# Softmax reciprocal on ScalarE, eight residuals by accumulating stores, and a third pairwise add of the logit products, in a fused attention-plus-GeGLU kernel

## Chip, cores and metric

The kernel runs on one core of one Trainium2 chip. The metric is the device time of one execution in microseconds, lower is better. Three runs of the kernel before gave 183.99, 184.02 and 184.84 us, the median is 184.02 us.

## What is computed

The input x has 2048 rows of 512 bfloat16 values. Its layer norm goes through two parallel branches, and both results are added to x:

```
xn = layernorm(x)
q, k, v = split(xn @ wqkv)                 # 32 heads of 16
logits[h, s, w] = q[h, s] . k[h, s - 2*w] / 4      # w = 0..7, masked where s - 2*w < 0
o[h, s] = sum over w of softmax_w(logits)[h, s, w] * v[h, s - 2*w]
A = o @ wo
B = (gelu(xn @ w_gate) * (xn @ w_up)) @ w_down      # inner width 1376
out = x + A + B
```

## The kernel before

**Tiling.** The 2048 rows are worked on in four blocks of 512 (b = 0 to 3), each of four tiles of 128 rows. Activations lie transposed (features on partitions, 512 rows along the free dimension), and matmuls are 128x128 by 128x512 in bfloat16 into one of eight PSUM banks.

**Names.** Every piece of work is a task with a name, a block number b and often a tile number. The tasks that matter here, with the engine that runs them:

- TensorE: `mm{b}_{0,1,2}_{g}` (line 1009) makes Q, K and V in four groups g; `fg{b}_{j}` and `fu{b}_{j}` (1217) make gate and up columns; `er{b}_3` (1085) sums the logit products over the partitions of a head by a matmul with a 0/1 matrix; `acc..{t}` (1302) makes the output tile t from both branches, in one bank. The parts `accw12` to `accw15` are the attention share of the last block and are kept for the end.
- ScalarE: `evq`, `evk`, `evv` (1020), `gelu` (1227), `uev` (1234) and `fe` (1335) empty PSUM banks; `exp{b}` (1131) is the exponential of the softmax; `bnst`, `bnag`, `sub`, `norm` and small ones are the layer norm of later blocks.
- VectorE: `pr{b}_{g}` (1040) multiplies Q by eight shifted copies of K (4096 elements per partition, float16); `pa{b}_0` and `pa{b}_1` (1053) add the four products in pairs; `d1`, `d2` (1117, 1122) subtract the maximum of the logits; `d4a`, `d4b`, `d4c` (1138) sum the eight exponentials; `d5` (1150) is the reciprocal of that sum; `d6` (1155) multiplies; `pv`, `pw`, `pz` (1184, 1193, 1199) weight V and sum into OT; `h` (1241) multiplies gelu by up; `fin` (1340, 1346) adds the residual x.
- SyncE issues all DMAs: loads, `ss`/`sl` (1164, 1176), which send the softmax weights to DRAM and bring them back spread over partitions, the transposing `trx` (882), the residual loads `ldxr` (1288) and the stores `sto` (1353).
- GpSimd makes constants at the start and a power per pair of tiles (`sq`, 832).

**What sets the order.** The order of the tasks on each engine is written out by hand in `ORDER` (line 404), one list for each engine, and each engine runs its list strictly in sequence. `Graph.schedule` (207) only gives out the buffer slots in that order, and `assign_sync` (317) puts semaphore waits where a task reads, overwrites or reuses what another engine made. So a task that waits holds back everything behind it on its engine. Buffers that tie the engines together are the eight PSUM banks (the two of the logits are held from `er` to `exp`), three slots each for gelu and up tiles (freed by `h`), and four output tiles OB (written by `fe`, freed when the store has landed).

**The softmax of one block** runs `er` on TensorE, `d1` and `d2` on VectorE, `exp` on ScalarE, `d4a`, `d4b`, `d4c`, `d5`, `d6` on VectorE, then `ss`, `sl`, `pv`, `pw`, `pz`. In the third and fourth block, as in the others, `er` takes two rounds of eight matmuls, one for each pair sum:

```
hhs = (0,) if b in PR_ADD3 else (0, 1)
```

with `PR_ADD3` empty. ScalarE works from tables of functions: gelu and exp lie in different ones, and a switch is an instruction of its own, which the build puts ahead of the first activation that needs it. The kernel before has ten such loads.

**Residuals.** For each of the 16 output tiles SyncE loads 128 rows of x (`ldxr`), `fe` copies the bank to OB (14 tiles), `fin` adds x on VectorE, and SyncE stores the tile (`sto`).

Of the kernel before, what the change touches and what calls it, by code (L numbers as in the profile page):

```python
# [12 lines left out]
    DMA_ISSUE=0.48,  # L13
    DMA_FIXED=2.0,
# [121 lines left out]
class Graph:  # L136
# [70 lines left out]
    def schedule(self, orders, params=None):  # L207
# [59 lines left out]
        for _ in range(len(self.tasks)):  # L267
# [23 lines left out]
            elif t.eng == "pe":  # L291
                sw = 0.0
                if t.mode is not None:
                    if pe_mode not in (None, t.mode):
                        sw = prm["PE_MODE_SWITCH"]
                    pe_mode = t.mode
                t.end = est + sw + pe_clock.run(est, t.dur, t.util)
                t.done = t.end + prm["PE_DRAIN"]
            else:
                t.end = est + t.dur  # L300
                t.done = t.end + prm["DRAIN"]
                if t.eng == "act" and t.table is not None:
                    act_table = t.table
# [13 lines left out]
    def assign_sync(self, cnt_sems, dma_sems):  # L317
        order = self.order
        for e in ("pe", "act", "dve", "pool"):
            for i, t in enumerate(order[e]):  # L320
                t.seq = i + 1
                t.sem = cnt_sems[e]
                t.val = i + 1
# [3 lines left out]
        for t in order["sp"]:  # L327
# [6 lines left out]
            dlast[si] = t  # L334
        self.dma_totals = [(dma_sems[i], dcount[i]) for i in range(len(dma_sems)) if dcount[i] > 0]
        know = {e: {} for e in ENGS}
        allt = sorted((t for t in self.tasks if not t.dropped), key=lambda t: (t.start, t.idx))
        for t in allt:
            K = know[t.eng]
            deps = list(t.deps)  # L340
            if t.eng == "sp" and t.prev_on_sem is not None:
                deps.append(t.prev_on_sem)
# [21 lines left out]
    def emit_engine(self, eng_name, e):  # L364
# [7 lines left out]
        for t in self.order[eng_name]:  # L372
# [4 lines left out]
            if eng_name == "sp" and t is self.order["sp"][-4]:  # L377
                late = self.order["sp"][-7:]
                for (s, tot) in self.dma_totals:
# [3 lines left out]
            ins.then_inc(t.sem, 16 if eng_name == "sp" else 1)  # L383
# [5 lines left out]
    def report(self):  # L389
# [18 lines left out]
        "mm0_2_0_0 mm0_2_3_0 mm0_2_2_0 mm0_2_1_0 fg0_0 fg0_1 fg0_2 fu0_0 fg0_3 fu0_1 fu0_2 fg0_4 fu0_3 fg0_5 "  # L408
        "fu0_4 fu0_5 fg0_6 fg0_7 er0_3 mm1_0_0_0 mm1_1_0_0 mm1_0_1_0 mm1_1_1_0 fg1_0 fu0_6 mm1_0_3_0 "
        "mm1_0_2_0 mm1_1_3_0 fu0_7 fu1_0 fg1_1 fg0_8 fu1_1 mm1_1_2_0 fu0_8 mm1_2_0_0 fg1_2 fg0_9 fu1_2 "  # L410
        "mm1_2_2_0 fg1_3 fu1_3 fu0_9 fg0_10 fg1_4 fu1_4 mm1_2_3_0 fg1_5 mm1_2_1_0 fg1_6 fu1_5 fu1_6 fg1_7 "
        "mm2_0_0_0 mm2_1_1_0 mm2_1_0_0 mm2_0_3_0 er1_3 mm2_0_1_0 fg1_10 mm2_1_2_0 mm2_2_1_0 mm2_0_2_0 fu1_7 "
        "fg2_0 accd1 mm2_1_3_0 accd2 fg2_1 mm2_2_3_0 mm2_2_2_0 fg1_8 fg2_2 acca0 fu2_0 accb0 fg1_9 mm2_2_0_0 "
        "accd3 er2_3 fu2_1 fu1_8 fu1_9 fu2_2 fg2_3 fu2_3 mm3_1_2_0 mm3_1_1_0 mm3_1_3_0 mm3_0_1_0 mm3_0_0_0 "
        "fg2_4 mm3_1_0_0 fu2_4 mm3_0_2_0 fg3_0 mm3_0_3_0 fu3_0 fg3_1 fg2_10 fg3_2 accd7 accd5 mm3_2_0_0 "
        "fg2_5 fu3_1 fg3_3 mm3_2_3_0 mm3_2_1_0 fu2_5 fu3_2 acca4 er3_3 accb4 fg3_4 accd6 fu3_3 fu3_4 fg2_6 "
        "fg3_5 fu2_6 fg2_7 fg3_6 fu2_7 fg2_8 fu2_8 fu3_5 fg3_7 fu3_6 mm3_2_2_0 fg2_9 fu3_7 fu2_9 fg3_8 fu3_8 "
        "fg3_9 fg3_10 acca8 accd10 accd9 fu3_9 accb8 accd11 acca12 accd13 accd14_0 accd14_1 accw14_0 "
        "accw14_1 accw13 accb12 accd15_0 accw12 accw15_0 accd15_1 accw15_1 accd15_2 accw15_2",
    "act":  # L420
        "c_tbl sx1 sq0 negm1 sxx1 sq1 evx0_0 evx0_1 evq0_0 sq2 evq0_1 evk0_0 evx1_0 sq3 evk0_1 bnst8 evx1_1 "
        "bnst9 evq0_2 sq6 evk0_2 evq0_3 evk0_3 ve8 evv0_0_0 sq4 vp8 bnag8 bnag9 va8 gelu0_0 evv0_2_0 "
        "evv0_3_0 bnst10 gelu0_1 bnst11 uev0_2 gelu0_3 vb8 gelu0_4 uev0_1 uev0_3 ve10 gelu0_5 uev0_4 uev0_0 "
        "uev0_5 gelu0_2 halo1 vp10 gelu0_7 bnag10 bnag11 evq1_0_0 evk1_0_0 evv0_1_0 evq1_1_0 evk1_1_0 "
        "gelu0_6 exp0 sub11 evq1_3_0 evk1_3_0 evq1_2_0 va10 uev0_7 uev1_0 uev0_10c uev0_6 sub9 vb10 sub8 "
        "uev1_1 evk1_2_0 norm9 uev0_10b gelu1_1 gelu1_0 norm8 gelu0_8 evv1_0_0 gelu1_2 sub10 uev0_8 bnst12 "
        "gelu0_9 norm11 uev1_2 uev0_9 norm10 evv1_2_0 gelu1_4 gelu1_3 uev1_3 evv1_1_0 uev1_4 uev1_5 uev0_10a "
        "bnst13 gelu1_5 gelu0_10 uev1_6 evk2_1_0 evv1_3_0 evk2_0_0 ve12 vp12 gelu1_7 bnag12 evq2_0_0 gelu1_6 "
        "evq2_1_0 uev1_10b bnag13 uev1_10c halv1 evk2_2_0 evq2_2_0 halo2 exp1 bnst14 sub12 bnst15 uev1_7 "
        "va12 ve14 vb12 uev1_10a vp14 bnag14 evk2_3_0 bnag15 evq2_3_0 evv2_1_0 va14 vb14 fe1 fe2 sub14 "  # L430
        "gelu2_0 evv2_2_0 halo3 gelu1_10 sub15 uev2_0 norm12 sub13 evv2_0_0 evv2_3_0 norm13 fe0 norm15 fe3 "
        "norm14 gelu1_8 gelu2_1 gelu1_9 uev2_1 uev1_8 uev2_2 uev1_9 uev2_3 gelu2_2 evk3_2_0 evk3_1_0 "
        "uev2_10b gelu2_3 exp2 evq3_1_0 evk3_3_0 evq3_2_0 evq3_0_0 halv2 evk3_0_0 uev2_10c evq3_3_0 uev2_4 "
        "uev2_10a gelu2_10 gelu3_1 uev3_0 gelu3_0 fe7 evv3_0_0 gelu2_5 gelu3_3 evv3_1_0 uev2_5 uev3_1 fe5 "
        "gelu2_4 gelu3_2 uev3_10c halv3 evv3_3_0 uev3_2 fe4 fe6 uev3_3 uev3_10b exp3 gelu3_5 uev2_6 gelu3_4 "
        "gelu2_7 uev2_7 uev2_8 gelu3_6 gelu2_6 evv3_2_0 gelu3_7 uev3_4 gelu2_8 gelu2_9 uev2_9 uev3_10a "
        "uev3_7 uev3_5 uev3_6 gelu3_10 fe10 gelu3_8 gelu3_9 uev3_9 fe9 uev3_8 fe8 fe11 fe13 fe12",
    "dve":
        "c_wdz bnst0 bnag0 sub0 rstd0 norm0 mean1 sub1 evy0_0 rstd1 norm1 evy0_1 bnst2 bnag2 sub2 rstd2 "
        "norm2 bnst3 bnag3 sub3 rstd3 norm3 bnst7 bnst6 bnst5 bnag6 bnag7 bnst4 bnag5 sub7 rstd6 bnag4 sub6 "  # L440
        "norm7 sub4 sub5 norm6 pr0_2 pr0_0 pr0_3 rstd4 pr0_1 norm4 norm5 pa0_1 pa0_0 h0_0 h0_1 h0_2 mask "
        "d1_0 d2_0 pr1_0 pr1_1 d4a_0 d4b_0 d4c_0 d5_0 rstd8 d6_0 pr1_3 pa1_0 pr1_2 h0_3 pa1_1 pv0_1 rstd10 "
        "pv0_3 h0_4 pv0_0 h1_1 pv0_2 pw0_1 h0_10 pw0_2 d1_1 pw0_3 d2_1 pz0 pr2_2 d4a_1 pr2_0 d4b_1 h1_3 "
        "d4c_1 h1_2 d5_1 h1_0 d6_1 pr2_1 pr2_3 pa2_0 fin1 rstd12 pa2_1 h1_10 pv1_1 rstd14 pv1_3 d1_2 pv1_0 "
        "d2_2 pv1_2 pw1_1 fin3 pw1_2 h2_1 pw1_3 h1_4 d4a_2 pz1 d4b_2 pr3_1 d4c_2 pr3_2 d5_2 fin0 d6_2 pr3_3 "
        "pr3_0 h2_0 h2_10 pa3_0 fin2 pa3_1 pv2_0 pv2_2 d1_3 pv2_1 d2_3 pw2_1 h3_1 d4a_3 h3_0 d4b_3 fin7 "
        "d4c_3 h2_2 d5_3 fin5 d6_3 pv2_3 pw2_2 h2_3 pw2_3 h2_4 pz2 fin4 pv3_3 pv3_0 pv3_1 fin6 pw3_1 fin10 "
        "h3_3 h3_10 pv3_2 h3_2 fin9 h3_4 pw3_2 fin8 pw3_3 fin11 pz3 fin14_0 fin14_1 fin13 fin15_0 fin15_1 "
        "fin12 fin15_2",
    "pool":  # L450
        "c_ones c_onef c_id c_vnpad c_idb c_eps c_mhalf c_e8a c_e8b c_e8c c_e8d c_ktpad c_mask0 c_mask1 "
        "c_utz sq8 sq10 sq12 sq14",
    "sp":
        "ld_x0_0 ld_x0_1 ld_wq ld_x1_0 ld_wk ld_x1_1 ld_wv ld_x2 ld_x4 ld_x3 ld_wg0 ld_wu0 ld_wt0 ld_x5 "
        "ld_wt1 trx3_0 ld_wt2 trx3_1 trx2_0 trx2_1 ld_wd0 ld_x6 ldxr1 ld_x7 ld_wd1 ld_wo ss0_2 ss0_3 ss0_0 "
        "ss0_1 ldxr2 sl0_1 sl0_3 sl0_2 trx4_0 sl0_0 trx4_1 trx5_1 trx5_0 ss1_2 ss1_3 ss1_1 ss1_0 sl1_1 sl1_3 "
        "sl1_0 sl1_2 ldxr3 trx6_0 trx6_1 trx7_1 trx7_0 sto3 sto1 ldxr0 ldxr7 ss2_1 ss2_2 ss2_3 ss2_0 sl2_0 "
        "sl2_3 sl2_2 sto0 sl2_1 sto2 ldxr5 ldxr4 sto5 ss3_0 ss3_1 ss3_2 ss3_3 ldxr10 sl3_3 sl3_0 sl3_2 sl3_1 "
        "ldxr6 sto4 sto6 ldxr8 ldxr9 sto9 ldxr11 ldxr14 sto8 sto7 sto10 ldxr13 sto11 sto14_0 sto14_1 ldxr15 "
        "ldxr12 sto13 sto15_0 sto15_1 sto12 sto15_2",  # L460
# [8 lines left out]
def d_act(n):  # L469
    return 0.10 + 0.00085 * n  # L470
# [10 lines left out]
def bass_parallel_sum__sliding_local_dilated__glu_gated_geglu__prompt_kernel(nc, A_x, A_wqkv, A_wo, B_x, B_w_gate, B_w_up, B_w_down, out, dbg=None, cfg=None):  # L481
# [42 lines left out]
    with contextlib.ExitStack() as es:  # L524
# [56 lines left out]
        cnt = {e: es.enter_context(nc.semaphore("cnt_" + e)) for e in ("pe", "act", "dve", "pool")}  # L581
        dsems = [es.enter_context(nc.semaphore("dma%d" % i)) for i in range(NDMASEM)]
# [360 lines left out]
        for b in range(NB):  # L943
# [185 lines left out]

            def mk_d3(lgv=lgv):  # L1130
                return lambda e: e.activation(out=EX[:, :], in_=lgv(0, 128, [(1, 1024)]), func=ACTF.Exp)
            G.task("act", "exp%d" % b, d_act(1024), mk_d3(), rd=[it_lg], wr=[it_ex], prio=base + 32,
                   table="exp", batch=b)
# [12 lines left out]

            def mk_d5(msv=msv, it=it_ms):
                def f(e):
                    with nc.allow_low_precision(reason="the reference holds the sums of exponentials in bf16"):
                        return e.reciprocal(out=rc[:, it.slot, :], in_=msv(1))  # L1150
                return f
            G.task("dve", "d5_%d" % b, 0.87, mk_d5(), rd=[(it_ms, 1)], wr=[(it_ms, 2)], prio=base + 34)
# [129 lines left out]

            for ti in range(4):
# [133 lines left out]
```

## Time and profile before

| what | us |
|---|---|
| median of three runs | 184.02 |
| the profiled execution, its own time | 184.58 |
| its span (first to last instruction) | 182.7 |
| TensorE busy | 178.9 (98%) |
| VectorE busy | 169.6 (93%) |
| ScalarE busy | 128.4 (70%) |
| GpSimd busy | 9.5 (5%) |
| granted TensorE clock | 1.00 throughout |

The times in the profile are of one execution, so they are compared with its own 184.58 us, of which 1.9 us lie outside the span. A busy share is an average over the whole span; the same engine can be full in one stretch and idle in another, and a table by stretches shows that. On ScalarE and VectorE an instruction starts about 0.1 us before the one ahead of it is over, so that a row of 0.60 us takes 0.49 us of the engine when the next one is ready. In the chain of work that ended last, each step is followed back to what released it.

### The profile page before, as it was taken

How to read it: one execution, taken by the hardware profiler on the slowest of the kernel's cores; microseconds unless marked ns; L12 is line 12 of the kernel's file. 1: busy time of each engine (PE TensorE's matmuls, PEld its weight loads, DVE VectorE, ACT ScalarE, POOL GpSimd, SP SyncE). 2: the span in 40 equal slices, each digit the busy share in tenths (PEclk: the TensorE clock that was granted, in tenths of full speed). 3: DMA queues.
4: the chain of work that ended last, by engine and by line, in shares of the span. 5: the costliest groups of instructions: out<-in, count | busy, mean ns of one | idle time of the engine just before them, and what ended most of it. 6: DMA issues, size and time to landing. Idle time of an engine off the chain costs nothing.

```text
span 182.7 us, 2790 instructions
## 1 busy us (share of the span) xinstructions
PE 178.9 (98%) x1068; PEld 90.6 (50%) x1068; DVE 169.6 (93%) x172; ACT 128.4 (70%) x258; POOL 9.5 (5%) x23
## 2 busy tenths in 40 slices
PE   8999999999999999999999999999999999999994
PEld 2886444544444444444444544444444444444664
DVE  3769999999999999999999999999999999999922
ACT  5688987999999899998695977527449764234011
POOL 6000010003300000122000000000000000000000
PEclk9999999999999999999999999999999999999999
DMA  4999905932562000002851020128000346022433
GB/s 125 360 376 381 125 18 118 367 127 49 183 145 57 0 0 4 0 12 76 256 62 30 4 82 0 30 62 285 28 0 0 92 131 213 0 86 61 140 104 100
DMA packets 26221, 19.60 MB, mean 107 GB/s; under 512 B 13825, under 2 KB 23009, under 8 KB 26209
## 3 DMA queue, kind: packets, MB, share of 16 engines
q1 hardware_dynamic: 26208, 19.44, 37.0%
q8 instruction: 8, 0.13, 0.3%
q14 instruction: 5, 0.03, 0.1%
HBM read 14.71 MB, written 3.15 MB: 98 GB/s over the span
## 4 chain that ended last, share of the span: by engine, by line
PE 91%; DMA 4%; SPq 2%; ACT 1%; issue 0%; DVE 0%; DVEq 0%
PE PS L1217 38%; PE PS L1302 28%; PE PS L1009 19%; DMA XIN<-in_A_x_dram 4%; PE PS L1256 2%; PE PS L1085 2%; PE PS L1078 1%; PE PS L959 1%; SPq L731 1%; SPq L687 1%; ACT XS L769 0%; SPq L737 0%; ACT xnT L919 0%; DVE OB L1346 0%; DVEq L376 0%
## 5 line engine op out<-in xcount | busy, mean ns | idle before, releaser
L1302 PE MATMUL PS<-Wd,HT 128*128 128x512 bf16 (+2 forms) x209 | 41.0, 346 | 0.0
L1217 PE MATMUL PS<-xnT,Wg 128*128 128x512 bf16 x160 | 39.8, 379 | 0.0
L1217 PE MATMUL PS<-xnT,Wu 128*128 128x512 bf16 x160 | 39.1, 379 | 0.0
L1009 PE MATMUL PS<-xnT,Wqkv 128*128 128x512 bf16 x160 | 38.0, 380 | 0.0
L1184 DVE TENSOR_TENSOR UNI<-VN,PT 128x4096 f16<-128x4096 bf16 x16 | 36.3, 2287 | 0.0
L1040 DVE TENSOR_TENSOR UNI<-QT,KT 128x4096 f16<-128x4096 bf16 x16 | 36.1, 2286 | 0.0
L1302 PEld LDWEIGHTS PS<-Wd,HT 128*128 128x128 bf16 x209 | 19.6, 98 | 19.2 <-issue 0.4
L1234 ACT ACTIVATE UU<-PS 128x512 bf16<-128x512 f32 x40 | 23.1, 600 | 6.4 <-PE PS L1217 6.1
L1193 DVE TENSOR_TENSOR UNI<-UNI 128x4096 f16<-128x4096 f16 x12 | 27.5, 2290 | 0.0
L1227 ACT ACTIVATE GG<-PS 128x512 bf16<-128x512 f32 x40 | 22.9, 602 | 5.9 <-DVE HT L1241 5.8
L1009 PEld LDWEIGHTS PS<-xnT,Wqkv 128*128 128x128 bf16 x160 | 17.9, 113 | 16.9 <-issue 0.8
L1217 PEld LDWEIGHTS PS<-xnT,Wu 128*128 128x128 bf16 x160 | 15.6, 98 | 19.0 <-ACT XIN L853 0.4
L1217 PEld LDWEIGHTS PS<-xnT,Wg 128*128 128x128 bf16 x160 | 15.7, 98 | 18.7
L1335 ACT ACTIVATE OB<-PS 128x512 bf16<-128x512 f32 x14 | 8.3, 601 | 17.3 <-PE PS L1302 15.1
L1053 DVE TENSOR_TENSOR UNI<-UNI 128x4096 f16<-128x4096 f16 x8 | 18.2, 2286 | 0.0
L1302 PE MATMUL PS<-Wo,OT 128*128 128x512 bf16 (+2 forms) x76 | 16.5, 346 | 0.0
L1020 ACT ACTIVATE VN<-PS 128x512 bf16<-128x512 f32 x16 | 9.3, 597 | 6.5 <-PE PS L1009 6.5
L1241 DVE TENSOR_TENSOR HT<-GG,UU 128x1024 bf16<-128x1024 bf16 x20 | 13.6, 686 | 0.0
L832 POOL TENSOR_TENSOR sq<-ve,mhalf 128x2 bf16<-128x2 f32 x4 | 6.6, 1657 | 72.8 <-ACT ve L828 72.8
L1302 PEld LDWEIGHTS PS<-Wo,OT 128*128 128x128 bf16 x76 | 7.1, 98 | 6.6 <-issue 0.3
L1272 ACT ACTIVATE UT<-PS 64x256 bf16<-64x256 f32 (+1 forms) x12 | 5.4, 447 | 6.7 <-PE PS L1256 3.9
L959 PE MATMUL PS<-xnT,Wqkv 128*128 128x128 bf16 x128 | 8.3, 222 | 0.3 <-ACT xnT L919 0.2
(85 smaller groups left out, 159.5 us busy)
## 6 DMA issues: line engine op xcount, KB each, us to landing
PT<-pt_scratch SPq DMA_DIRECT2D x16, 256.0 KB, 4.2
XR<-in_A_x_dram SPq DMA_DIRECT2D x16, 128.0 KB, 2.2
out_dram<-OB SPq DMA_DIRECT2D x14, 128.0 KB, 1.9
Wqkv<-in_A_wqkv_dram SPq DMA_DIRECT2D x3, 512.0 KB, 5.0
XIN<-in_A_x_dram SPq DMA_DIRECT2D x6, 256.0 KB, 6.7
Wg<-in_B_w_gate_dram SPq DMA_DIRECT2D x1, 1280.0 KB, 8.6
Wu<-in_B_w_up_dram SPq DMA_DIRECT2D x1, 1280.0 KB, 11.6
Wd<-in_B_w_down_dram SPq DMA_DIRECT2D x1, 1280.0 KB, 6.6
```

The costliest lines, as they stand in the source:

```text
L959: ins = e.matmul(PS[:, 512 * it.slot + 128 * g:512 * it.slot + 128 * g + 128], lhsT=wcols(which, kt, g), rhs=xnT[:, itx.slot, kt, t * 128: ...
L1009: ins = e.matmul(PS[:, 512 * it.slot:512 * it.slot + 512], lhsT=wcols(which, kt, g), rhs=xnT[:, itx.slot, kt, :], start=(kt == 0), stop=(k ...
L1020: return e.activation(out=o, in_=PS[:, 512 * it.slot:512 * it.slot + 512], func=ACTF.Identity, scale=(QSC, 1.0, 1.0)[which])
L1040: return lambda e: e.tensor_tensor(out=UNI[:, it.slot, :, :], in0=bass.AP(QT, (itq.slot * 4 + g) * 512, [[NQT * 4 * 512, 128], [0, 8], [1, ...
L1053: return lambda e: e.tensor_tensor(out=UNI[:, i0.slot, :, :], in0=UNI[:, i0.slot, :, :], in1=UNI[:, i1.slot, :, :], op=ALU.add)
L1184: return lambda e: e.tensor_tensor(out=bass.AP(UNI, ito.slot * 4096, [[NUNI * 4096, 128], [2048, 2], [512, 4], [1, 512]]), in0=bass.AP(VN, ...
L1193: return lambda e: e.tensor_tensor(out=UNI[:, i0.slot, :, :], in0=UNI[:, i0.slot, :, :], in1=UNI[:, i1.slot, :, :], op=ALU.add)
L1217: ins = e.matmul(PS[0:M, 512 * it.slot:512 * it.slot + 512], lhsT=Wx[:, kt, j * 128:j * 128 + M], rhs=xnT[:, itx.slot, kt, :], start=(kt = ...
L1227: return lambda e: e.activation(out=GG[:, ito.slot, q, :], in_=PS[:, 512 * it.slot:512 * it.slot + 512], func=ACTF.Gelu_apprx_tanh)
L1234: return lambda e: e.activation(out=UU[:, ito.slot, q, :], in_=PS[:, 512 * it.slot:512 * it.slot + 512], func=ACTF.Identity)
L1241: return lambda e: e.tensor_tensor(out=HT[:, ito.slot, j - 1:j + 1, :], in0=GG[:, ig.slot, :, :], in1=UU[:, iu.slot, :, :], op=ALU.mult)
L1302: ins = e.matmul(PS[:, 512 * it.slot:512 * it.slot + CW], lhsT=(OT[:, ito.slot, q, ti * 128:(ti + 1) * 128] if kind == "o" else HT[:, ith. ...
```

## The change

Three edits, and with them a new order of all tasks.

1. **Softmax reciprocal.** `d5` leaves VectorE. ScalarE takes the logarithm of the sum (`ln{b}`, in place) and then the exponential with scale -1 (`d5_{b}`), 128 elements per partition each. A one-element logarithm (`pre{b}`) stands ahead of `exp{b}`. In the list of ScalarE other tasks stand between `ln` and `d5`.
2. **Residuals of tiles 0 to 7.** One DMA of SyncE for each of the first two blocks (`prx0`, `prx1`) copies 512 rows of x from DRAM to the output in DRAM. The eight tiles are then stored by GpSimd with a DMA that adds to what lies there (`sta{t}`); each waits for its `fe` and for the copy. Eight `ldxr`, eight `fin` and eight `sto` are gone. The stores have six semaphores of their own, on which SyncE waits near the end.
3. **Third pairwise add.** In the third and fourth block `pa{b}_2` adds the two pair sums on VectorE, and `er{b}_3` takes one round of eight matmuls in place of two.

The diff, cut to its core; of the order, the parts that are used below:

```diff
@@ ORDER, pe
-"fu3_9 accb8 accd11 acca12 accd13 accd14_0 accd14_1 accw14_0 accw14_1 accw13 accb12 accd15_0 ..."
+"fu3_9 acca8 accb8 accd9 accd10 accd11 acca12 accd13 accd14_1 accd14_0 accw14_0 accw14_1 accw13 accd15_0 ..."
@@ ORDER, act
-"... evk1_0_0 evv0_1_0 evq1_1_0 evk1_1_0 gelu0_6 exp0 sub11 evq1_3_0 evk1_3_0 evq1_2_0 va10 uev0_7 uev1_0 "
-"uev0_10c uev0_6 sub9 vb10 sub8 uev1_1 evk1_2_0 norm9 uev0_10b gelu1_1 gelu1_0 norm8 gelu0_8 ..."
+"... gelu0_7 gelu0_6 halo1 evq1_0_0 evq1_1_0 evk1_1_0 pre0 exp0 evq1_3_0 evk1_3_0 bnag11 uev0_6 evk1_2_0 ln0 "
+"va10 d5_0 uev1_0 vb10 evq1_2_0 sub8 uev0_7 gelu0_8 gelu1_1 sub10 gelu0_9 uev0_8 gelu1_0 ..."
...
+"... evk2_2_0 gelu0_10 bnag12 evq2_2_0 evv2_2_0 bnag13 evq2_0_0 pre1 exp1 sub12 bnst14 uev1_10c evv2_3_0 "
+"bnst15 evq2_1_0 va12 evq2_3_0 vb12 ve14 ln1 uev1_10b d5_1 ... gelu1_10 ..."
+"... uev2_4 pre2 evk3_1_0 exp2 evq3_1_0 evk3_3_0 evq3_3_0 evv3_1_0 evk3_0_0 gelu3_0 ln2 d5_2 fe7 fe6 uev3_0 "
+"gelu3_2 ... fe4 pre3 exp3 evv3_3_0 uev3_3 uev3_4 uev3_10b uev2_6 ln3 halv3 d5_3 gelu2_8 ..."
@@ ORDER, dve
-"d1_0 d2_0 pr1_0 pr1_1 d4a_0 d4b_0 d4c_0 d5_0 rstd8 d6_0 pr1_3 pa1_0 pr1_2 h0_3 pa1_1 pv0_1 ..."
+"d1_0 d2_0 pr1_0 pr1_1 d4a_0 d4b_0 rstd8 d4c_0 pr1_3 d6_0 pa1_0 pr1_2 h0_3 pa1_1 rstd10 h0_4 h1_0 "
+"pv0_0 ... pw0_3 d1_1 h0_10 pz0 d2_1 pr2_0 d4a_1 pr2_2 d4b_1 h1_1 d4c_1 pr2_1 d6_1 pr2_3 pa2_0 pa2_1 h1_3 pa2_2 ..."
+"... d4c_2 pr3_0 d6_2 ... pa3_1 pa3_0 h2_0 pa3_2 pv2_0 d1_3 pv2_1 d2_3 pw2_1 d4a_3 h3_0 d4b_3 h2_2 d4c_3 pv2_2 d6_3 ..."
@@ ORDER, pool
-"c_utz sq8 sq10 sq12 sq14",
+"c_utz sq8 sq10 sq12 sq14 sta1 sta0 sta2 sta7 sta5 sta4 sta3 sta6",
@@ emit_engine
+                for q in self.acc_last:
+                    e.wait_ge(q.sem, q.val)
@@ parameters
+    FIN3 = cfg.get("FIN3", tuple(range(8)))
-    PR_ADD3 = cfg.get("PR_ADD3", ())
+    PR_ADD3 = cfg.get("PR_ADD3", (2, 3))
@@ softmax
+            t_pre = G.task("act", "pre%d" % b, 0.2, lambda e: e.activation(
+                out=onef[:, 1:2], in_=onef[:, 0:1], func=ACTF.Ln), rd=[(I_onef, 0)], wr=[(I_onef, 1)],
+                prio=base + 32, table="exp")
...
+            def mk_ln(msv=msv):
+                return lambda e: e.activation(out=msv(1), in_=msv(1), func=ACTF.Ln)
...
             def mk_d5(msv=msv, it=it_ms):
-                def f(e):
-                    with nc.allow_low_precision(reason="the reference holds the sums of exponentials in bf16"):
-                        return e.reciprocal(out=rc[:, it.slot, :], in_=msv(1))
-                return f
-            G.task("dve", "d5_%d" % b, 0.87, mk_d5(), rd=[(it_ms, 1)], wr=[(it_ms, 2)], prio=base + 34)
+                return lambda e: e.activation(out=rc[:, it.slot, :], in_=msv(1), func=ACTF.Exp, scale=-1.0)
+            G.task("act", "d5_%d" % b, 0.21, mk_d5(), rd=[(it_ms, 1)], wr=[(it_ms, 2)], prio=base + 34, table="exp")
@@ residuals
+            if 4 * b in FIN3:
+                def mk_px(b=b):
+                    return lambda e: e.dma_start(out2[512 * b:512 * b + 512, :], x2[512 * b:512 * b + 512, :])
+                t_px = G.task("sp", "prx%d" % b, 0, mk_px(), wr=[(I_out, b)], prio=base + 58, nbytes=512 * 1024)
...
+                        if t in FIN3:
+                            def mk_ao(t=t, ito=it_ob):
+                                return lambda e: e.dma_start(out2[128 * t:128 * t + 128, :], OB[:, ito.slot, :],
+                                                             accum_op=ALU.add)
+                            G.task("pool", "sta%d" % t, 4.0, mk_ao(), rd=[it_ob, (I_out, t // 4)], prio=base + 62,
+                                   nbytes=128 * 1024)
+                            continue
```

The instructions as built from the changed kernel, ScalarE's around the softmax of block 0 (a `LoadActFuncSet` is a table load; lines of the changed kernel):

```
53 L1032 Activation KT<-PS 128x512
54 L1142 LoadActFuncSet
55 L1142 Activation onef<-onef 128x1
56 L1147 LoadActFuncSet
57 L1147 Activation EX<-PS 128x1024
58 L1032 Activation QT<-PS 128x512
59 L1032 Activation KT<-PS 128x512
60 L827 Activation XS,s<-XIN,nmean 128x512
61 L1252 Activation UU<-PS 128x512
62 L1032 Activation KT<-PS 128x512
63 L1165 LoadActFuncSet
64 L1165 Activation ms<-ms 128x128
65 L812 Activation vb<-s 128x2
66 L1169 LoadActFuncSet
67 L1169 Activation rc<-ms 128x128
```

In all, the changed kernel has 23 such loads: the first two as before, then five, five, six and five in the four blocks (in the third, `gelu3_0` stands between `exp2` and `ln2`).

## The prediction

> **What bounds the kernel now.** I read the page first: busy shares, then the chain that ended last.
>
> ```profile
> PE 178.9 (98%) x1068; PEld 90.6 (50%) x1068; DVE 169.6 (93%) x172; ACT 128.4 (70%) x258; POOL 9.5 (5%) x23
> ...
> PE 91%; DMA 4%; SPq 2%; ACT 1%; issue 0%; DVE 0%; DVEq 0%
> ```
>
> TensorE (PE) is the chain: from 12.9 to 180.3 us it hardly waits. The table by stretches shows how near the other two are (columns: stretch, its length, busy time of PE, weight loads, DVE, ACT, POOL).
>
> ```profile
> 37.00:50.00 13.00, 13.00 (x62) 6.26 (x61) 12.89 (x13) 12.88 (x23) 2.84 (x1) 1.00 0.36 110
> 50.00:72.00 22.00, 22.00 (x128) 10.56 (x127) 21.86 (x15) 20.33 (x45) 0.00 (x0) 1.00 0.21 46
> 72.00:98.00 26.00, 26.00 (x147) 11.98 (x146) 25.74 (x23) 22.55 (x46) 3.08 (x2) 1.00 0.33 77
> 98.00:120.00 22.00, 22.00 (x104) 10.53 (x103) 22.00 (x20) 15.22 (x26) 0.00 (x0) 1.00 0.10 30
> ```
>
> ScalarE (ACT), 70% on average, is all but full from 37 to 98 us, where the first two softmaxes lie; VectorE (DVE) is full throughout. Next the timeline of ACT around the first exponential (start, duration).
>
> ```profile
> 35.73 0.60 ACT L1020 ACTIVATE KT<-PS 128x512 bf16<-128x512 f32 x1
> 36.23 0.59 ACT L1227 ACTIVATE GG<-PS 128x512 bf16<-128x512 f32 x1
> 36.84 1.28 ACT L1131 ACT_TABLE_LOAD   x1
> 38.13 1.02 ACT L1131 ACTIVATE EX<-PS 128x1024 f16<-128x1024 f32 x1
> ```
>
> A table load takes 1.31 us from the end of one activation to the start of the next. Last, the groups with their shapes kept apart, and the timeline of the end.
>
> ```profile
> L1053 DVE TENSOR_TENSOR UNI<-UNI 128x4096 f16<-128x4096 f16 x8 | 18.2, 2286 | 0.0
> L1131 ACT ACT_TABLE_LOAD x4 | 5.1, 1283 | 0.1
> L1085 PE MATMUL PS<-UNI,E 128*32 128x512 f16 x64 | 4.2, 379 | 0.0
> L1150 DVE RECIPROCAL rc<-ms 128x128 f16<-128x128 f32 x4 | 3.8, 950 | 0.0
> ```
>
> ```profile
> 172.03 1.23 DVE L1199 TENSOR_TENSOR OT<-UNI 128x2048 bf16<-128x2048 f16 x1
> 173.63 1.51 PEld L1302 LDWEIGHTS PS<-Wo,OT 128*128 128x128 bf16 x12
> 173.74 1.90 PE L1302 MATMUL PS<-Wo,OT 128*128 128x256 bf16 x12
> ```
>
> DVE finishes the last `pz` at 173.26, and PE takes the first attention matmul of the last block (`accw14_0`) 0.48 us later. So two chains of equal length end here: PE's own work, and DVE's. After that both have 6.5 us of PE work (173.74 to 180.25) and the tail.
>
> **What the Trainium skill says.** "ScalarE: Activation LUTs", section "Table sets: the hidden batching unit": ln and then exp need one load, since one set holds both. The built order does not show this: each of `pre`, `exp`, `ln`, `d5` has its own load. Its section "What ACT_TABLE_LOAD costs" gives 1283 ns and a drain of 1380 ns; the trace agrees on the 1283 but shows 1.31 us in all, and I take that. The same section's price for an activation with immediate operands, 186 ns + 0.833 ns per column, makes 0.29 us for 128 columns (an estimate; the trace has 0.38 us for 256). "DMA: Bandwidth & Descriptors", section "SWDGE vs HWDGE vs iDMA": an accumulating DMA must be issued by GpSimd, which writes its descriptors in software. No row of before shows one.
>
> **The change part by part.**
>
> *Third add.* PE loses 2 x 8 of 64 matmuls of L1085, 4.2 us x 16/64 = 1.05; in the chain 16 of them take 0.86, so 2 x 0.43 = 0.86 us, all on PE's path. DVE gains two adds of 2.29 us that start 2.20 apart: +4.4.
>
> *Residuals.* DVE loses 8 x 0.34 us (L1340, start to start) = 2.7. SyncE loses 8 loads and 8 stores and gains two copies; no wait in the chain ended with these, so I take zero. `prx` waits only for `gelu0_5` and `gelu1_5`, and these are over long before `ss0` and `ss1` behind it. GpSimd's eight stores stand behind its last power, so no layer norm is delayed; SyncE's new wait for them stands ahead of its fourth last DMA, after the block-3 tiles, when they are over. What hides them is the OB slots: `fe7` needs the slot of `sta1`, some 20 us later; the tightest is `fe4` after `sta7`, some 12 us. Bounds for one store: 1.9 us (the median of SyncE's) to 12 us; I take less than 12, hence nothing. Beyond it ACT, and the banks behind it, waits for the excess.
>
> *Reciprocal.* DVE loses 4 x 0.87 (start to start) = 3.5. ACT gains 13 loads (23 against 10) x 1.31 = 17.0 us and 4 x 3 small activations of some 0.2 = 2.4: 128.4 becomes about 148, still under the span. But where do they fall? Per block about 4.5 us, in blocks 0 and 1 inside the full stretch.
>
> Block 0. `evk1_1_0` follows PE and starts at 35.73 in either order (the PE work ahead of it is the same), over at 36.33. Load, ln, load: 36.33 + 1.31 + 0.30 + 1.31 = 39.25; `exp0` to 40.27 (before: 39.15). Then three evacuations, `bnag11` and another evacuation (4 x 0.49 + 0.83) end at 43.06; load 1.31, `ln0` 0.30, `va10`, load 1.31, `d5_0` 0.29: 46.4. `d6_0` starts at 46.45 in place of 41.47. DVE has only `pr1_3` (2.2 us, moved ahead of it) to fill this, so it loses 2.8.
> The same delay reaches PE: after `d5_0` five tasks (2.3 us) and the load back (1.4) put `gelu0_8` at 50.0 to 50.6. `fu1_2` wants its bank. PE's work summed in the new order (0.865 us per four matmuls) would be there at 47.4: PE stands 3.2 us.
>
> Block 1. With PE 3.2 late, ACT follows at `evq2_2_0` (72.3); 5.3 us of tasks and two loads later `exp1` is at 77.65 to 78.7 (before: 73.0 to 74.0). DVE's own sum from `d6_0` would be at `d4a_1` at 77.7: waits 1.0. `ln1`, `d5_1` with their loads end at 86.45; DVE would be at `d6_1` at 84.5: waits 2.0.
>
> Block 2. ACT has more room (15.2 of 22 us), `d4a_2` is two adds and more behind `d2_2`, and both sums reach `d6_2` at 124.4: zero (up to 0.8).
>
> Block 3. `ln3` comes after `uev2_6`, which needs `h2_2` just ahead of `d4c_3`: about 146.0, then load, ln, `halv3`, load, exp: 149.6. DVE would be there at 147.8: waits 1.8.
>
> Sum for DVE from `d6_0` to the last `pz`: 45 big operations x 2.203 = 99.1; 3 `pz`, 3 `d1`, 3 `d2` of 1.14 to 1.15 = 10.3; three `d4` sets of 0.75 and four `d6` of 0.60 = 4.6; `h` 17 x 0.605 + 4 x 0.34 = 11.7; four `fin`, three `rstd` 1.6: 127.3. (The same sum in the old order gives 130.3 against 130.56 measured.) So `pz3` starts at 46.45 + 127.3 + 1.0 + 2.0 + 1.8 + 0.2 (`d1_1` waits for the late PE) = 178.7 and ends at 180.0, against 173.26: 6.7 later. PE, with its stalls of 3.2 at `fu1_2`, 1.4 more at `acca0` (bank of `uev1_7`) and 1 more up to 112 us, is some 5.6 - 0.9 = 4.7 behind, so it is PE that waits for `pz3`, and the rest follows unchanged. The profiled execution would be 184.58 + 6.7 = 191.3; the median lies 0.56 lower, so 190.7.
>
> **Rivals.**
> *A, the above: 190.7* (189 to 192.5). For it: DVE has no slack at `accw14_0`, and ACT none from 37 to 98.
> *B, PE's own stalls decide: 184.02 + 4.7 = 188.7* (186.5 to 189). The waits at `d6` could be shorter where ACT catches up earlier; DVE would then be there in time. For it: blocks 2 and 3 rest on long sums. Against: `d6_0` rests on a short one.
> *C, the delays feed back: about 194* (192.5 to 197). A late `h` holds gelu (L1227 already waits 5.8 us for it), that holds a bank, PE stands, and the next softmax starts later: a second round of the first stall, some 3 us more. An accumulating store beyond 12 us would come in here too. Against: the slots of gelu come free 1 to 7 us before their use in my sums, except two in block 2 (`gelu2_10`, `uev2_10c`).
> *D, not slower: 184.02 - 0.86 = 183.2* (182.7 to 184.0). One mechanism: ACT, between `pre` and `d5`, pays only one load for a softmax, because the second, third and fourth find both functions in the active set. It decides from 2.4 loads (3.2 us) saved of the three extra ones in block 0, since then `gelu0_8` is ready when `fu1_2` comes. Against: the build has 23 loads, and the ten that the build has of before are the ten in its trace (4 + 4 + 2).
>
> **How the numbers follow.** About 0.5% (0.9 us) can be told from no change. A 0.52, B 0.18, C 0.23, D 0.07. D is split: faster by over 0.5% 0.03, within 0.5% 0.04; slower 0.93. The range, 186.8 to 195.0, holds A, most of B and two thirds of C; it takes in the 0.8 of block 2 and leaves out D and stores above 12 us.
>
> **What would show it.** Right: 13 more table loads; ACT busy near 147 us; PE idle ahead of L1217's successor around 47 to 51 us, released by ACT's gelu; DVE idle ahead of `d6` in blocks 0, 1 and 3, some 2.8, 2 and 1.8 us, released by ACT; `pz` of the last block over near 180. Third add: L1085 with 48 matmuls, the adds with 10. Wrong: under 23 loads; no idle DVE at `d6`; or `fe` waiting for GpSimd's stores, which I price at nothing.

## The result and the profile after

The changed kernel takes 191.57 us (median of four runs, 191.43 to 192.09) against 184.05 us for the kernel before beside it: a ratio of 1.040, 95% interval 1.037 to 1.044. The profiled execution took 191.61 us with a span of 189.9, so 7.0 us more than the 184.58 of the execution profiled before. 190.7 was predicted.

The page after, busy shares and the chain by engine:

```profile
PE 177.6 (94%) x1035; PEld 88.5 (47%) x1052; DVE 168.4 (89%) x162; ACT 146.6 (77%) x283; POOL 16.8 (9%) x31
...
PE 45%; ACT 33%; DVE 11%; DMA 6%; SPq 2%; issue 2%; DVEq 0%
```

ACT rose from 128.4 to 146.6 us, and the chain, 91% PE before, now runs a third of its way through ACT. No engine is full over the whole span: the time is lost in waits. The table by stretches (same columns as before) shows where they are:

```profile
37.00:50.00 13.00, 10.95 (x49) 4.52 (x47) 10.27 (x10) 12.87 (x22) 2.73 (x1) 1.00 0.07 16
50.00:72.00 22.00, 21.61 (x123) 10.26 (x126) 22.00 (x15) 20.74 (x46) 0.00 (x0) 1.00 0.37 99
72.00:98.00 26.00, 25.05 (x114) 11.39 (x116) 22.82 (x19) 25.59 (x51) 4.48 (x3) 1.00 0.22 56
98.00:120.00 22.00, 21.18 (x117) 9.98 (x117) 22.00 (x18) 19.33 (x35) 1.73 (x2) 1.00 0.31 37
...
145.00:163.00 18.00, 15.95 (x74) 7.12 (x74) 16.14 (x14) 14.44 (x26) 0.00 (x0) 1.00 0.27 74
```

PE, which was busy for the whole of each stretch before, stands 2.0 us in the first and 2.0 in the last (here too it was busy for all 18.00 before); DVE stands 2.7, 3.2 and 1.9 in three of them. ACT's timeline around the first softmax (start, duration; in brackets the idle before a row and what ended it):

```profile
35.56 0.60 ACT L1032 ACTIVATE KT<-PS 128x512 bf16<-128x512 f32 x1 [0.27 <-PE PS L1021]
36.18 1.28 ACT L1142 ACT_TABLE_LOAD   x1
37.47 0.20 ACT L1142 ACTIVATE onef<-onef 128x1 f32<-128x1 f32 x1
37.69 1.28 ACT L1147 ACT_TABLE_LOAD   x1
38.98 1.02 ACT L1147 ACTIVATE EX<-PS 128x1024 f16<-128x1024 f32 x1
...
42.67 1.28 ACT L1165 ACT_TABLE_LOAD   x1
43.97 0.31 ACT L1165 ACTIVATE ms<-ms 128x128 f32<-128x128 f32 x1
44.18 0.19 ACT L812 ACTIVATE vb<-s 128x2 bf16<-128x2 f32 x1
44.39 1.28 ACT L1169 ACT_TABLE_LOAD   x1
45.68 0.31 ACT L1169 ACTIVATE rc<-ms 128x128 f16<-128x128 f32 x1
```

Four loads for one softmax, two of them one after the other around a logarithm of a single element. The groups, with shapes kept apart (busy, mean ns, idle before and its releaser):

```profile
L1065 DVE TENSOR_TENSOR UNI<-UNI 128x4096 f16<-128x4096 f16 x10 | 22.6, 2283 | 0.0
L1365 POOL DMA_DIRECT2D out_dram<-OB x8 | 7.1, 1042 | 43.7 <-ACT OB L1359 41.4 <-ACT XIN L858 2.2
L1097 PE MATMUL PS<-UNI,E 128*32 128x512 f16 x48 | 3.3, 379 | 0.0
L1173 DVE TENSOR_TENSOR PB<-EX,rc 128x1024 bf16<-128x1024 f16 x4 | 2.8, 692 | 7.0 <-ACT rc L1169 7.0
```

DVE has two adds more (18.2 to 22.6 us), PE 16 matmuls fewer (4.2 to 3.3), and `d6` (L1173) makes DVE wait 7.0 us for ACT's reciprocal, 0.0 before. The end:

```profile
178.83 1.22 DVE L1217 TENSOR_TENSOR OT<-UNI 128x2048 bf16<-128x2048 f16 x1
...
180.77 1.51 PEld L1326 LDWEIGHTS PS<-Wo,OT 128*128 128x128 bf16 x12
180.88 1.90 PE L1326 MATMUL PS<-Wo,OT 128*128 128x256 bf16 x11
```

The last `pz` is over at 180.04, but PE takes `accw14_0` only at 180.77, after 9 us of matmuls without a gap. So PE did not wait for `pz3`. What made PE late, the fourth block shows best:

```profile
143.54 1.04 PE L1235 MATMUL PS<-xnT,Wu 128*128 128x512 bf16 x4 [0.71 <-ACT EX L1147]
...
149.43 0.31 ACT L1169 ACTIVATE rc<-ms 128x128 f16<-128x128 f32 x1
149.76 1.28 ACT L1245 ACT_TABLE_LOAD   x1
149.77 0.69 DVE L1173 TENSOR_TENSOR PB<-EX,rc 128x1024 bf16<-128x1024 f16 x1 [1.86 <-ACT rc L1169]
...
151.05 0.60 ACT L1245 ACTIVATE GG<-PS 128x512 bf16<-128x512 f32 x1
...
151.70 0.60 PE L1235 MATMUL PS<-xnT,Wg 128*128 128x512 bf16 x2 [1.94 <-ACT GG L1245]
```

First PE stands 0.71 us (at `fu2_6`) for a logits bank, which is free only after `exp3`, and `exp3` stands behind two loads. Then ACT needs two loads for `ln3` and `d5_3` and a third to come back to gelu; `gelu2_8` behind them frees a PSUM bank at 151.65, and PE has stood 1.94 us for that bank (at `fg3_6`). DVE waited 1.86 us for the first two of these three loads.

### The profile page after: what moved, and what is told of

It is laid out like the page before. It is cut to its first block, busy times and chain, and to the rows that moved or that the text cites. A ratio compares the mean times of both kernels' runs of the same rounds, so it can differ in the third digit from the quotient of the medians.

```text
span 189.9 us, 2754 instructions
## 1 busy us (share of the span) xinstructions
PE 177.6 (94%) x1035; PEld 88.5 (47%) x1052; DVE 168.4 (89%) x162; ACT 146.6 (77%) x283; POOL 16.8 (9%) x31
## 4 chain that ended last, share of the span: by engine, by line
PE 45%; ACT 33%; DVE 11%; DMA 6%; SPq 2%; issue 2%; DVEq 0%
PE PS L1235 16%; PE PS L1326 14%; PE PS L1021 13%; DVE UNI L1065 3%; DMA XIN<-in_A_x_dram 3%; ACT GG L1245 3%; ACT L1165 3%; DMA xnT<-XIN 3%; ACT UU L1252 2%; ACT L1169 2%; DVE UNI L1202 2%; ACT QT L1032 2%; ACT L1245 2%; ACT XS L827 2%; ACT KT L1032 2%
## 5 line engine op out<-in xcount | busy, mean ns | idle before, releaser
L1235 PE MATMUL PS<-xnT,Wg 128*128 128x512 bf16 x157 | 38.7, 380 | 3.4 <-ACT GG L1245 1.9
L1235 PE MATMUL PS<-xnT,Wu 128*128 128x512 bf16 x154 | 38.2, 380 | 2.1 <-ACT GG L1245 0.9
L1021 PE MATMUL PS<-xnT,Wqkv 128*128 128x512 bf16 x155 | 36.9, 379 | 0.9 <-DMA xnT<-XIN 0.6
L1211 DVE TENSOR_TENSOR UNI<-UNI 128x4096 f16<-128x4096 f16 x12 | 27.4, 2280 | 0.0
L1235 PEld LDWEIGHTS PS<-xnT,Wg 128*128 128x128 bf16 x160 | 15.2, 98 | 23.1 <-ACT GG L1245 2.4
L1065 DVE TENSOR_TENSOR UNI<-UNI 128x4096 f16<-128x4096 f16 x10 | 22.6, 2283 | 0.0
L1365 POOL DMA_DIRECT2D out_dram<-OB x8 | 7.1, 1042 | 43.7 <-ACT OB L1359 41.4
```

Source lines behind the costliest of these rows:

```text
L1021: ins = e.matmul(PS[:, 512 * it.slot:512 * it.slot + 512], lhsT=wcols(which, kt, g), rhs=xnT[:, itx.slot, kt, :], start=(kt == 0), stop=(k ...
L1065: return lambda e: e.tensor_tensor(out=UNI[:, i0.slot, :, :], in0=UNI[:, i0.slot, :, :], in1=UNI[:, i1.slot, :, :], op=ALU.add)
L1211: return lambda e: e.tensor_tensor(out=UNI[:, i0.slot, :, :], in0=UNI[:, i0.slot, :, :], in1=UNI[:, i1.slot, :, :], op=ALU.add)
L1235: ins = e.matmul(PS[0:M, 512 * it.slot:512 * it.slot + 512], lhsT=Wx[:, kt, j * 128:j * 128 + M], rhs=xnT[:, itx.slot, kt, :], start=(kt = ...
```

## The experiments

Three theories (their letters are not those of the rivals in the prediction). **P**: the 13 added loads hold ACT's evictions back, PE waits for banks, and these waits set the end, with DVE's chain 0.4 to 0.8 us behind. **D**, as predicted: DVE's waits at `d6` carry the last `pz`, and PE waits for it. **O**: the loads are hidden, and the new order, the third add or the accumulating stores carry the loss. Each time stands beside the median of the kernel before in the same set of runs (184.3 to 184.5 us).

**1. One set for Ln and Exp.** The Trainium skill, "ScalarE: Activation LUTs", section "Table sets: the hidden batching unit", states that one set holds both functions. In the changed kernel each of `pre`, `exp`, `ln` and `d5` has a load of its own, even `ln2` and `d5_2`, which stand next to each other in its list (only in the other three blocks are there tasks between the two). So the sets that it loads do not hold both. Here that set is loaded by hand, and `gelu3_0` is moved so that it no longer parts `exp2` from `ln2`.

```diff
+                    e.preload_act_table_set("natural_log_exp_and_others")
                     return e.activation(out=onef[:, 1:2], in_=onef[:, 0:1], func=ACTF.Ln)
@@ ORDER, act
-... evk3_0_0 gelu3_0 ln2 d5_2 fe7 ...
+... evk3_0_0 ln2 d5_2 gelu3_0 fe7 ...
```

> The changed kernel, but with one table set that serves Ln and Exp loaded explicitly ahead of the small Ln, and gelu3_0 moved behind d5_2: 10 table loads in place of 23, everything else as it is. Theory P (the 13 added loads hold evictions back, PE waits for PSUM banks, and its own bank waits set the end; DVE's chain follows 0.4 to 0.8 us behind): the idle of PE at fu1_2, acca0, fu2_6 and fg3_6 goes but for some tenths, what stays is the transposes (0.6) less the cheaper er (0.9), and DVE's chain, with 4.4 added, 2.7 and 3.5 to 3.8 taken away, ends before 173: 183 to 185 us. Theory O (order, third add or accumulating stores carry the loss): over 188. A middle value (185 to 188) would say that the round trip DVE to ACT to DVE costs by itself, loads apart.

Measured: 183.49 us (22 runs), ratio 0.9955 (0.9943 to 0.9967). The page and the end of this kernel:

```profile
PE 178.0 (98%) x1052; PEld 90.2 (50%) x1052; DVE 168.1 (93%) x162; ACT 130.1 (72%) x270; POOL 25.2 (14%) x31
...
PE 92%; DMA 3%; SPq 2%; ACT 1%; issue 0%; DVE 0%; DVEq 0%
```

```profile
170.82 1.23 DVE L1221 TENSOR_TENSOR OT<-UNI 128x2048 bf16<-128x2048 f16 x1
172.43 1.51 PEld L1330 LDWEIGHTS PS<-Wo,OT 128*128 128x128 bf16 x12
172.54 1.90 PE L1330 MATMUL PS<-Wo,OT 128*128 128x256 bf16 x12
```

Some 8 us are gone with the loads (experiment 6 shows the same without the move of `gelu3_0`), the chain is PE again, and the trace has no idle of PE over 0.1 us between 13 and 179 us. O falls. The Trainium skill's statement holds here, once the set is asked for: ten loads, as before the change, for softmaxes that take both functions. This is the fastest kernel of the study, 0.3 to 0.6% under the kernel before.

**2. The reciprocal back on VectorE**, everything else as changed.

```diff
-            G.task("act", "ln%d" % b, 0.21, mk_ln(), rd=[(it_ms, 1)], wr=[(it_ms, 1)], prio=base + 34, table="exp")
-            G.task("act", "d5_%d" % b, 0.21, mk_d5(), rd=[(it_ms, 1)], wr=[(it_ms, 2)], prio=base + 34, table="exp")
+            G.task("dve", "d5_%d" % b, 0.87, mk_d5(), rd=[(it_ms, 1)], wr=[(it_ms, 2)], prio=base + 34)
@@ ORDER, dve
-... d4c_0 pr1_3 d6_0 ...
+... d4c_0 d5_0 pr1_3 d6_0 ...
```

> The changed kernel with the first edit alone undone: reciprocal on DVE behind d4c, no pre, ln and d5 on ACT, 10 loads; new order, third add and accumulating stores stay. Theory P: DVE's five waits for exp and d5 (8.1 us in all) go and 3.8 us of reciprocals come back, pz3 at about 174.5, PE free of its bank waits: 184 to 185.5 us. Theory O: over 188. If it is as fast as the one with the joint set or faster, the reciprocal on ACT earns nothing even without its loads.

Measured: 187.25 us, ratio 1.015 (1.011 to 1.018); the estimate was 2 us low. The end:

```profile
175.30 1.22 DVE L1210 TENSOR_TENSOR OT<-UNI 128x2048 bf16<-128x2048 f16 x1
176.57 1.42 PEld L1319 LDWEIGHTS PS<-Wo,OT 128*128 128x128 bf16 x12 [0.32 <-DVE OT L1210]
```

Here PE does wait for `pz3`, 0.32 us, and 6.5 us of PE work follow as ever. DVE's `pz3` ends at 176.52 where 174.5 was expected: against experiment 1 it carries the reciprocals (3.8 us busy) and waits early on (it reaches the first mask 0.4 later, and `pv0_0` waits 1.03 for a DMA). So the reciprocal on ACT is worth up to 3.8 us in this kernel, if it needs no extra loads (some 1.4 of it may belong to these two waits, which were not tried apart); with 13 more loads it costs 4.3. With the reciprocal on DVE the rest of the change is 2.9 us slower than the kernel before, which fits what is left on DVE: 4.4 us of adds more, 2.7 of residuals less, and these waits.

**3. Loads without the wait of `d6`.** The reciprocal is on DVE as in 2; ACT still runs `pre`, and a one-element Ln and Exp, which nobody reads, in the places of `ln` and `d5`.

```diff
+            G.task("act", "ln%d" % b, 0.21, lambda e: e.activation(
+                out=onef[:, 2:3], in_=onef[:, 0:1], func=ACTF.Ln), ...)
+            G.task("act", "dx%d" % b, 0.21, lambda e: e.activation(
+                out=onef[:, 3:4], in_=onef[:, 0:1], func=ACTF.Exp), ...)
```

> Reciprocal on DVE as in the last, but ACT still runs a 1-column Ln and a 1-column Exp in the places of ln and d5, on constants that nobody reads, so that all 23 loads stay and nothing on DVE waits for them. Theory P (PE's bank waits carry the end, not DVE's wait for d5): PE's idle stays, 189.5 to 191.6 us. Theory D (as predicted: d6's wait on DVE and then pz3 carry it): pz3 at about 175.5, so 185 to 187 us.

Measured: 191.24 us, ratio 1.037 (1.033 to 1.041), not to be told from the changed kernel's 1.040. What PE waited for, and the end:

```profile
PE PS L1241 <- ACT GG L1251: 2.5, 2, 1.6
PE PS L1241 <- ACT EX L1147: 0.9, 2, 0.7
PE PS L1241 <- ACT UU L1258: 0.9, 1, 0.9
```

```profile
177.68 1.22 DVE L1223 TENSOR_TENSOR OT<-UNI 128x2048 bf16<-128x2048 f16 x1
180.13 1.51 PEld L1332 LDWEIGHTS PS<-Wo,OT 128*128 128x128 bf16 x12
```

(Columns of the first: waited for, us in total, times, longest.) `pz3` is done at 178.90, and PE comes 1.2 us later by its own lateness. P holds, D falls: with no wait at `d6` at all, the time stays, and PE does not wait for `pz3`. (`pz3` itself comes only 1.1 us earlier than in the changed kernel, not at 175.5: DVE has its reciprocals back and waits 1.37 us for an eviction and 1.36 for `exp1`.)

**4. Without the third add**, PE takes two logit passes again.

```diff
-    PR_ADD3 = cfg.get("PR_ADD3", (2, 3))
+    PR_ADD3 = cfg.get("PR_ADD3", ())
@@ ORDER, dve
-... pa2_1 h1_3 pa2_2 rstd12 ... h2_0 pa3_2 pv2_0 ...
+... pa2_1 h1_3 rstd12 ... h2_0 pv2_0 ...
```

> The changed kernel without the third pairwise add in blocks 2 and 3: DVE has 4.4 us less, PE 0.86 more for the second logit pass. Theory P (PE's own chain sets the end at 180.8, pz3 0.8 earlier is no cause): 190.8 to 192.5 us, PE going on without a wait into accw14_0 long after pz3. Theory D (pz3 sets the end, PE waits): pz3 at 174.5 to 176, end set by PE's remaining waits at what was predicted for them, about 188.5 to 189.6 us.

Measured: 191.80 us, ratio 1.042 (1.038 to 1.045). 4.4 us less on DVE bring nothing, as P says and D does not. But `pz3` did not come earlier either, which both theories expected:

```profile
179.05 1.22 DVE L1217 TENSOR_TENSOR OT<-UNI 128x2048 bf16<-128x2048 f16 x1
...
181.00 1.51 PEld L1326 LDWEIGHTS PS<-Wo,OT 128*128 128x128 bf16 x12
```

It is over at 180.27, where it was over at 180.04 with the adds. DVE's idle between 37 us and `pz3` rose from 8.1 to 12.3 us: what it no longer adds, it waits for ACT, PE and DMAs. So DVE's end follows the late engines here and not its own work, and PE again comes 0.7 us after it. PE's extra 0.86 hardly shows either (+0.2): its idle falls from 6.7 to 5.7 us, so PE works where it would have waited.

**5. The joint set in the fourth block only.**

```diff
+                    if b == 3:
+                        e.preload_act_table_set("natural_log_exp_and_others")
```

> The changed kernel with the joint table set loaded ahead of the small Ln in the fourth block only: 20 loads in place of 23, and none between exp3 and d5_3; blocks 0 to 2 keep theirs. It asks the step that failed, that the loads of the fourth block cost PE nothing. Theory P: the idle of PE ahead of fu2_6 (0.7) and most of that ahead of fg3_6 (1.9) goes, pz3 comes 2 to 3 us earlier by the shorter waits for exp3 and d5_3: 188.3 to 189.5 us. If the step held (PE loses nothing there), PE's part stays and the time is 191 or more.

Measured: 189.03 us, ratio 1.025 (1.022 to 1.027): three loads of 23 removed give back 2.5 of 7.5 us. Both idles of PE in that block are gone, and the end turns over:

```profile
177.00 1.24 DVE L1222 TENSOR_TENSOR OT<-UNI 128x2048 bf16<-128x2048 f16 x1
178.29 1.42 PEld L1331 LDWEIGHTS PS<-Wo,OT 128*128 128x128 bf16 x12 [0.23 <-DVE OT L1222]
```

Now PE waits for `pz3`. The two chains are so close that removing the loads of one block changes which of them ends last.

**6. The joint set in every block, `gelu3_0` left where it was**: 13 loads.

```diff
+                    e.preload_act_table_set("natural_log_exp_and_others")
                     return e.activation(out=onef[:, 1:2], in_=onef[:, 0:1], func=ACTF.Ln)
```

> The changed kernel with the joint table set loaded ahead of the small Ln in each block, nothing moved: 13 loads, the three extra ones in the third block, where gelu3_0 stands between exp2 and ln2. Theory P prices a load by what is due behind it: nothing of PE's is late in the third block (no idle of PE from 107 to 136 in the changed kernel but for 0.16), d6_2 waits up to 0.5 on DVE: 183.3 to 184.3 us. If every load costs alike (7.3 / 13 = 0.56 us each): 183.5 + 3 x 0.56 = 185.2.

Measured: 183.79 us, ratio 0.9976 (0.9965 to 0.9987), against 0.9955 with ten loads: three loads for some 0.3 us, at the limit of what the intervals part. ACT in the third block of this kernel:

```profile
111.75 0.60 ACT L1032 ACTIVATE QT<-PS 128x512 bf16<-128x512 f32 x1 [1.67 <-PE PS L1021]
...
116.23 1.28 ACT L1169 ACT_TABLE_LOAD   x1
...
117.85 1.28 ACT L1173 ACT_TABLE_LOAD   x1
```

ACT had stood 1.67 us just ahead, waiting for PE; no eviction that PE needs is late behind these loads, and only `d6_2` waits (0.70). Through DVE a part of this comes to the end: `pz3` is over at 173.12, against 172.05 in experiment 1, and PE waits 0.23 us for it. So a load of 1.3 us costs 0.1 us here and 0.8 us in the fourth block.

**7 and 8. The first edit alone, in the old order**, with `pre`, `ln` and `d5` put by hand where their data come: once with the loads as built (22), once with the joint set (10). On VectorE `pr1_3` and `pr2_1` were moved ahead of `d6`.

```diff
@@ ORDER, act of the kernel before, + the new tasks
... pre0 exp0 sub11 evq1_3_0 evk1_3_0 ln0 evq1_2_0 va10 d5_0 ...
... bnag14 ln1 evk2_3_0 d5_1 ... uev2_10a ln2 d5_2 ... pre3 exp3 ln3 d5_3 gelu3_5 ...
```

> The kernel before with the first edit alone: pre, ln and d5 on ACT, in the old order with the new instructions put where their data come, 22 loads, no third add, residuals as before. DVE loses 3.8 us of reciprocals, ACT gains 12 loads. Theory P (the loads carry the whole loss): 189 to 193 us, with idle of PE ahead of matmuls that wait for evictions. Theory O (the new order, third add or stores carry it): 183.5 to 186 us.

> The kernel before with the first edit alone, as in the run with 22 loads, but with the joint set: 10 loads, order the same as there. Theory P: PE of the kernel before is without idle, DVE 3.8 shorter is no gain: 183.7 to 185.0 us, so that 12 loads alone make the difference to 201.6. If the old order, or the places of ln and d5 on ACT, caused those 201.6: over 188.

Measured: 201.51 us (ratio 1.091, 1.087 to 1.094) and 186.90 us (1.014, 1.011 to 1.017). Twelve loads are all that differs: 14.6 us, 1.2 each. Both exceed what was expected. With the joint set, `ln3`, set directly behind `exp3`, made ACT stand 1.83 us for `d4c_3`, and PE stood 1.87 us for the gelu behind it. That points to my placing and not to the edit; another place was not tried. With 22 loads PE stood 11.8 us and twice ran at half clock for a while (last columns of a stretch: granted clock, DMA share, GB/s):

```profile
86.00:88.70 2.70, 0.95 (x4) 0.27 (x5) 1.10 (x3) 2.69 (x6) 0.00 (x0) 0.85 0.01 3
88.70:90.00 1.30, 1.30 (x4) 0.48 (x5) 1.30 (x1) 1.27 (x5) 0.37 (x1) 0.50 0.21 50
...
154.50:158.20 3.70, 0.00 (x0) 0.00 (x0) 2.64 (x4) 3.64 (x6) 0.00 (x0) 1.00 0.24 73
...
160.00:162.00 2.00, 2.00 (x6) 0.75 (x5) 1.44 (x1) 1.51 (x4) 0.00 (x0) 0.50 0.48 106
```

Over the profiled execution, the longest of six with 202.72 us, the clock was 0.974, which is 5 us of its span of 200.7; in the other five it was 0.982 to 0.991, so about 2 to 4 us of the 14.6 are lost clock (estimates from these shares). The new order thus does not cause the loss: with 23 loads PE stands 6.7 us in it, never over 2, and keeps its clock at 1.00.

**9 and 10. The other two edits alone, in the old order**: the third add (`pa2_2` behind `pa2_1`, `pa3_2` behind `pa3_1`), and the residuals (no `ldxr`, `fin`, `sto` for tiles 0 to 7; `prx0`, `prx1` ahead of `ss0`, `ss1`; stores in the order of `fe`).

```diff
-    PR_ADD3 = cfg.get("PR_ADD3", ())
+    PR_ADD3 = cfg.get("PR_ADD3", (2, 3))
...
+    FIN3 = cfg.get("FIN3", tuple(range(8)))
```

> The kernel before with the third add alone in blocks 2 and 3, nothing else moved: DVE plus 4.4 us, PE minus 0.86. Two chains of equal length in the kernel before: DVE's carries on through, pz3 at 173.3 + 4.4 = 177.7, end 188.0 to 188.6 us. If DVE had slack that the profile doesn't show: 183.2 to 185.

> The kernel before with the second edit alone: the first eight residuals by copies into the output and accumulating stores from GpSimd, old order, no third add. DVE minus 2.7 us, ACT and PE as before. PE is without idle in the kernel before, so easing DVE alone gives nothing: 183.5 to 184.6 us. If the stores hold an output buffer or a queue: over 185, with a wait of ACT ahead of its output evictions.

Measured: 188.94 us (1.025, 1.022 to 1.027) and 184.22 us (0.9991, 0.9977 to 1.0004). Together they bear out the two equal chains of the kernel before: 4.4 us put on DVE cost 4.4, and 2.7 us taken from it bring nothing. In experiment 9 PE did not only wait at the end: it stood 1.66 us for an eviction that itself waited for DVE's `rstd`, 1.46 for a pair sum and 0.82 for an OT, all late work of DVE, so that both chains again meet (`pz3` over at 177.86, `accw14_0` at 177.92).

**11 and 12. Two edits taken out of the ten-load kernel**: the third add, and the residuals (`ldxr`, `fin` and `sto` of tiles 0 to 7 set back into the queues by hand).

```diff
-    PR_ADD3 = cfg.get("PR_ADD3", (2, 3))
+    PR_ADD3 = cfg.get("PR_ADD3", ())
...
-    FIN3 = cfg.get("FIN3", tuple(range(8)))
+    FIN3 = cfg.get("FIN3", ())
```

> The changed kernel with the joint set and gelu3_0 behind d5_2 (10 loads, 183.5 us), less the third add: DVE 4.4 shorter, PE 0.86 longer. There PE runs without idle from 12.9 to 179.0, so only PE's part counts: 184.1 to 184.7 us. If DVE's chain had set the end: faster than 183.5.

> The same 10-load kernel (183.5 us) with the first eight residuals back as loads, adds on DVE and plain stores, set into the queues by hand: DVE 2.7 longer. Its pz3 ends at 172.1, some 0.4 before PE needs it; so 2.3 us come through: 185.3 to 186.3 us. If DVE had more slack than that: under 184.5.

Measured: 184.41 us (1.0006, 0.9992 to 1.0019) and 185.86 us (1.008, 1.007 to 1.009), so 0.9 and 2.4 us more than experiment 1. Without the joint set's help the third add costs 4.4 us (9); with the reciprocal and eight residuals off DVE it saves 0.9; in the changed kernel it does neither (4).

## Why the prediction was right, and the step that failed

**The time** was right to 0.9 us, for a mechanism that was right in its cause and wrong in its last link. That it came so near is in part luck: the chain that was summed for it, DVE's, ended where it was said to, but another one set the end, and that one happens to be only 0.7 us longer.

**Reciprocal, right.** 13 more loads (23 of 1283 ns), ACT at 146.6 against about 148; an Ln or Exp of 128 columns took 0.31 us where 0.29 was estimated. `exp0` started at 38.98 (39.25 said), `d5_0` ended at 45.99 (46.4), `d6_0` started at 46.02 (46.45). DVE's waits: 2.70 (2.8) at `d6_0`, 1.18 (1.0) at `d4a_1`, 2.00 (2.0) at `d6_1`, 0.39 (0 to 0.8) at `d6_2`, 1.86 (1.8) at `d6_3`. `pz3` ended at 180.04 (180.0).

**Third add, right in its sizes.** DVE +4.4 and PE -0.9 on the page; alone it costs 4.4 (9), in the ten-load kernel it brings 0.9 (11). In the changed kernel neither reached the end (4), since both engines wait there anyway.

**Residuals, right at nothing on PE's path.** GpSimd's store took 1.04 us of GpSimd and landed 3.5 us after its issue in the median; no store from OB took longer than 4.7, under the 12 that would have held an OB slot, and `fe` waited for PE only.

**The step that failed** is in the sum for PE: "some 5.6 - 0.9 = 4.7 behind, so it is PE that waits for `pz3`". The kernel of experiment 1 runs PE's list in the same order and does not wait, so late means here: the start of a task less its start in that kernel. Up to 112 us the sum holds: PE was 2.9 late after `fu1_2` (3.2 said, in one wait; it was three), 4.4 from `acca0` (4.6) and 5.3 at `er3_3` (5.6). For the fourth block I charged the loads to DVE alone. They also held a logits bank until `exp3` (`fu2_6`, another 0.9) and the bank of `gelu2_8` behind the load back (`fg3_6`, another 2.1). So PE is 8.3 late at `accw14_0` (180.77 against 172.43), and 7.1 behind the kernel before (180.88 against 173.74) where 4.7 stood, and it reaches `accw14_0` 0.7 us after `pz3`. A transpose that PE waited for (0.56 us at 106, counted in the 5.3) was not foreseen either; experiment 2, with ten loads, has the same wait (0.55), and its cause was not tried.

So rival B's mechanism, PE's own bank waits, decided, at rival A's time: B's 188.7 was short by the 2.4 us of that block. Experiment 5 shows the missing term: without the loads of that block both waits are gone, 2.5 us come back, and PE then does wait for `pz3`. Experiments 3 and 4 agree: without the waits at `d6`, or with 4.4 us less for DVE to do, there is no gain, and PE still comes 1.2 and 0.7 us after `pz3`. Rival D's mechanism does not occur in this build, but was sound: when the second function is in the active set, the change is faster than the kernel before (183.49 us; 183.2 was said).

## What to carry to other kernels

Count the table loads in the built instructions, and ask of each what eviction stands behind it and whose bank that frees: the same 1.3 us cost 0.1 us where the engine had been waiting, 0.8 where an eviction that PE needed stood behind it, and 1.2 in an order that was not made for it. When two chains end within half a microsecond of each other, sum both up to the end with the same care, since every step that you charge to one can be owed by the other as well. Try a change together with what pays for it: the third add is 4.4 us worse alone and 0.9 better where VectorE has been relieved.

## What was not expected of the hardware

In the run with 22 loads TensorE lost clock after it had stood still. The Trainium skill, "TensorE: Matmul & The Clock Gate", section "HAM oscillation — how this bites in real kernels", warns of idle gaps over about 3.4 us. The run with 22 loads agrees: after 3.77 us of idle at 154.5 the clock was 0.50 from 160 to 162 us. It had also fallen during the second of two shorter waits, of 1.28 and 1.75 us with 1 us of work between them (the stretch from 86.0 to 88.7 has 0.85, the next one 0.50); a single wait of 1.94 us in the changed kernel, and one of 1.87 us in the run with the joint set, left it at 1.00. Because of this, stalls of one engine can cost more than their own length.
